# Spectral mixing and SwiGLU on one core: the transforms' first step on 32x32 parts of folded rows, its stores from SyncE

## The chip, the core and the metric

The kernel runs on one core of a Trainium2 chip, in fp32. The metric is the time of one execution on the device in microseconds (us), as the median of several runs. Engines are named as in the profile: PE is TensorE's matmul, PEld its weight load, DVE is VectorE, ACT is ScalarE, POOL is GpSimd, SP is SyncE. ACTq and SPq are the queues on which ACT and SP issue DMA transfers.

## The reference

Eight batches of 3008 tokens with 256 channels are filtered along the tokens and then go through a SwiGLU network with 1536 hidden columns:

```python
X = np.fft.rfft(x, axis=1)                     # x is (8, 3008, 256)
y = np.fft.irfft(X * (filt_r + 1j * filt_i)[None], n=3008, axis=1)
t = y.reshape(24064, 256)
g = t @ w_gate
out = (g / (1 + exp(-g)) * (t @ w_val)) @ w_out
```

## The kernel before, in words

Each batch is worked off in twelve steps: four token groups times three groups of hidden columns. A step runs through one list that is written out by hand, `SCHEDULE`, some 200 tokens long, and every engine keeps the order of its instructions in that list. The tokens that the text meets are these. `P`, `Q`, `A`, `B` and `E` are products of the gate and value matrices (L1075, PSUM tiles wk, wa, we). `W` is an output projection (L1172, tiles wA, wF, wG), and `o` adds such a tile into the output sums on DVE. `f`, `c`, `x`, `y`, `m`, `g`, `u`, `h` evict and combine the products (L1090 to L1122); `D` is such a combination on POOL. `z` transposes output sums. The large matmul work is cut by schemes of sums, so that a projection or a product has to wait for sums on DVE, ACT or POOL.

The filter of a batch is calculated while the network of the batch before it runs. Its transform is split over the factors 3008 = 47 x 64. A piece of that work is a generator, and each of the tokens `b0` to `b7` takes it on by one `yield`; these are the bursts. For batches from 2 on, steps 0 to 3 of the batch before hold `quads(0)` to `quads(3)`, the first step of the transform: 47-point sums down the rows, for two of the eight pieces of columns at a time. Each piece is 4 columns n of 256 channels, in two halves h that lie 32 columns apart. The burst b0 of a `quads` has eight matmuls (L716, PSUM tiles wqa), each with 47 rows times 64 results times 512 columns in a 64x64 part of the array; an fp32 matmul makes two passes, so the trace has 16 records. b1 and b2 each evict half h = 0 of a piece by an ACT copy (L725), then take the difference and the sum with half h = 1 on DVE (L331 and L328, helpers for all such sums). b3 and b4 store the pieces in DRAM from ACT's queue (L733), and `load_x` (L641) brings pieces for the next `quads` on SP. At b6 of step 3 `load_four` reads that DRAM tile for the second step of the transform, `fours`, which occupies steps 4 to 10 (matmuls L775 and L787); in it `keep` copies a PSUM tile on ACT (L801) and the copies' halves are swapped by DMA (the raw swaps). Scratch rows for all this lie in one tile, `lent`, and `room_of(tag)` gives the part of a tag (x, f, y, g, e, t).

PSUM tiles named w share seven banks in rotation: what asks for a bank waits until the reader of the bank's previous tile is done.

SP issues nearly all other transfers in the program's order, a transfer that has to wait holding those behind it. `reload_weights` (L493) brings the weights of the next step in pieces of 896 and 768 KB, each when PE is done with the piece it replaces. In batch 1, at places in steps 0 to 2 (`FILTER_AT`), `keep_filter` arranges the filter in DRAM, and `negated_filter` makes a copy of part of it with the sign turned: loads, an ACT multiplication (L323, 64x1024), and stores. Batch 0 takes other paths for its own transform and has weight preparation beside it; chores are pieces of work placed at a step and a token of batch 0.

Of the kernel before, what the change touches and what calls it, by code (L numbers as in the profile page):

```python
# [41 lines left out]
FP32 = mybir.dt.float32  # L42
# [57 lines left out]
S00 S01 W1 S20 S21 S10 S11 W5 o1 W2 o5 S30 S31 W6 o2 z0.o o6 W3 o3 z1.o x0.o x1.o x2.o x3.o x4.o  # L100
x5.o W7 q4 o7 z3.o W4 o4 z2.o X0.o X1.o X2.o X3.o X4.o X5.o
""".split()
FILTER_AT = ("f1", "P0", "Q2", "h0", "g3", "A12", "Q0", "P1", "c1", "h1")
BLOCKS = (0, 1, 3, 2)
PAIRS = ((0, 1), (1, 2), (2, 3), (0, 2), (1, 3), (0, 3))
PAIRS_USED = ((1, 3), (0, 1), (0, 2), (1, 2), (2, 3), (0, 3))
# [19 lines left out]
def dft_tables():  # L126
# [37 lines left out]
            if n >= NH:  # L164
                back[row:row + rows, first + N1 * i:first + N1 * (i + 1)] = one_hi[a:a + rows]

    quad = np.zeros((128, 64))
    for h, turn in enumerate((ph, ph + 2 * np.pi * s / (2 * N1))):
        cols = np.stack([np.cos(turn), -np.sin(turn)], 2).reshape(N1, 2 * NS)
        quad[64 * h:64 * h + N1, 0:2 * NS] = cols  # L170

    four = np.zeros((128, N_FOUR + 1, 2, 4, 64))
    lo, qq = np.arange(32), np.arange(32)
# [32 lines left out]
def kernel(  # L206
# [60 lines left out]
    def weights_of(b, k, g):  # L267
        return wt_1 if b == 0 and k < NT and g == 1 else wt_t

    dram_tiles = [wdpool.tile([2 * NS, N2, C], FP32, name=f"d{1 + i % 2}_{i // 2}")  # L270
                  for i in range(4)]
    yt_dram = [wdpool.tile([128, 3 * len(PAIRS), TQ], FP32, name=f"yt_{k}") for k in range(NT)]
    y_dram = [wdpool.tile([128, 8, TQ], FP32, name=f"y_{k}") for k in range(NCHUNK)]
    o_dram = [wdpool.tile([128, 4 * NH, RP], FP32, name=f"o_{k}") for k in range(NT)]
# [32 lines left out]

    def keep_filter(n):

        part, r, e, half = (0, 0, 1)[n // 4], (0, 1, 1)[n // 4], n // 2 % 2, n % 2  # L310
        q = 32 * e + 16 * half
        pin(nc.sync.dma_start(out=f_pairs[q:q + 16, r, part],
                              in_=filter_rows(part, e, half, 0, NS)))

    def negated_filter(w, stage):

        t = room_of("et"[w % 2])[0:64].rearrange("p (s c) -> p s c", c=C)
        if stage == 0:
            for q in range(4):
                pin(nc.sync.dma_start(out=t[16 * q:16 * q + 16],  # L320
                                      in_=filter_rows(1, q // 2, q % 2, 4 * w, 4)))
        elif stage == 1:
            pin(nc.scalar.mul(t, t, -1.0))  # L323
        else:
            pin(nc.sync.dma_start(out=f_pairs[:, 0, 1, 4 * w:4 * w + 4], in_=t))

    def add(eng, dst, a, b):
        return eng.tensor_tensor(out=dst, in0=a, in1=b, op=ALU.add)  # L328
# [246 lines left out]
    def load_back():  # L575

        t = rpool.tile([128, 2, 128], U32, name="quad", tag="pw", bufs=3)
        t = t.bitcast(FP32).rearrange("p b f -> p (b f)")
        quad_t.append(t)
        pin(nc.sync.dma_start(out=t[:, 0:64], in_=quad_dram.ap()))  # L580
# [19 lines left out]
    class Spectral:  # L600


        def __init__(self, b):
            self.b = b
            self.d1, self.d2 = [dram_tiles[2 * (b % 2) + i] for i in range(2)]
# [23 lines left out]
        def load_x(self, u):  # L629
            if self.b == 0:  # L630
                rows = x[0].rearrange("(r n) c -> r n c", n=32)
                for a, n in ((0, 4), (4, 4)):
                    for r in (slice(0, 80), slice(80, NR)):
                        self.load(out=x0[u][r, a:a + n, :],
                                  in_=rows[r, 8 * u + a:8 * u + a + n, :])
            elif self.b > 1:
                if u < N_QUAD:
                    self.x[u] = room_of("x", u).rearrange("p (n c) -> p n c", c=C)
                    rows = x[self.b].rearrange("(r n) c -> r n c", n=N2)
                    for h in range(2):  # L640
                        for a, e in ((0, 32), (32, N1)):  # L641
                            self.load(out=self.x[u][64 * h + a:64 * h + e],
                                      in_=rows[a:e, 32 * h + 4 * u:32 * h + 4 * u + 4])
            elif u < N_ONE:
                self.x[u] = xpool.tile([NR, NV, C], FP32, name=f"x_{self.b}_{u}", tag="x")
                rows = x[self.b].rearrange("(r n) c -> r n c", n=32)

                for r in (slice(0, 80), slice(80, NR)):
                    self.load(out=self.x[u][r], in_=rows[r, ts(u, NV), :])
# [49 lines left out]
        def bank(self, name):  # L699
# [2 lines left out]
                return bank(name).rearrange("p (i c) -> p i c", i=NV)  # L702
            return fbank(name)

        def quads(self, g):

            pieces = (2 * g, 2 * g + 1)
            banks = {}
            for u in pieces:
                xt = self.x.pop(u)  # L710
                for h in range(2):
                    banks[u, h] = bank(f"qa_{self.b}_{u}_{h}")
                for cp in range(2):
                    for h in range(2):
                        r = slice(64 * h, 64 * h + N1)
                        pin(nc.tensor.matmul(  # L716
                            out=banks[u, h][64 * cp:64 * cp + 64], lhsT=quad_t[0][r, 0:64],
                            rhs=xt[r, 2 * cp:2 * cp + 2].rearrange("p n c -> p (n c)"),
                            start=True, stop=True))
            yield  # L720
            t1 = {u: room_of("yg"[i]).rearrange("p (n h c) -> p n h c", h=2, c=C)
                  for i, u in enumerate(pieces)}
            for u in pieces:
                low, high = [banks[u, h].rearrange("p (n c) -> p n c", c=C) for h in range(2)]
                pin(nc.scalar.copy(out=t1[u][:, :, 0], in_=low))  # L725
                pin(sub(nc.vector, t1[u][:, :, 1], t1[u][:, :, 0], high))
                pin(add(nc.vector, t1[u][:, :, 0], t1[u][:, :, 0], high))
                yield
            d1 = self.d1.rearrange("a (n h) c -> a n h c", h=2)
            for u in pieces:  # L730
                for cp in range(2):
                    n = 4 * u + 2 * cp
                    pin(nc.scalar.dma_start(out=d1[:, n:n + 2], in_=t1[u][64 * cp:64 * cp + 2 * NS]))  # L733
                self.load_x(u + 2)
                yield
            if g == 3:
                self.load_filter(0)
                self.load_turns(0)
            yield
            if g == 3:  # L740
                self.load_four(0)

        def load_four(self, w):

            if w < N_FOUR:
                t = self.t2[w] = room_of("t").rearrange("p (s h c) -> p s h c", h=2, c=C)
                d1 = self.d1.rearrange("(s r) (n h) c -> s (r n) (h c)", r=2, h=2)
                for p in range(2):
                    s = 4 * w + 2 * p
                    self.load(out=t[64 * p:64 * p + 64].rearrange("p s h c -> p s (h c)"),  # L750
                              in_=d1[s:s + 2].rearrange("s q c -> q s c"))

        def load_filter(self, w):

# [10 lines left out]
        def fours(self, w):  # L765
# [32 lines left out]
            def keep(p):  # L798
                t = t1pool.tile([128, NV, C], FP32, name=f"raw_{self.b}_{w}_{p}", tag="t1", bufs=2)
                raw.append(t)  # L800
                pin(nc.scalar.copy(out=t, in_=there[p]))  # L801

            def real(p):
                a = slice(2 * p, 2 * p + 2)
# [576 lines left out]
    for b in range(B):  # L1381
# [36 lines left out]
        for step in range(NCHUNK * NG + (b == B - 1)):  # L1418
# [16 lines left out]
            for place, token in enumerate(SCHEDULE):  # L1435
# [31 lines left out]
                    continue  # L1467
                if b == 0 and (step, op) == (5, "A23"):
                    nxt.load_two(0)
                if b + 2 < B and (step, op) in ((11, "Q2"), (11, "B01")):  # L1470
                    following.load_x(int(op == "B01"))
                if b == 1 and step < 4 and op in FILTER_AT:
                    n = FILTER_AT.index(op)
                    if n < 4 and step < 3:
                        keep_filter(4 * step + n)
                    elif 4 <= n < 6 and step < 3:
                        negated_filter(2 * step + n % 2, 0)
                    elif n >= 6 and step:
                        negated_filter(2 * step - 2 + n % 2, n // 2 - 2)
# [43 lines left out]
```

## Time and profile before

| what | us |
|---|---|
| median of 3 runs | 2821.29 |
| lowest and highest run | 2817.37, 2822.79 |
| the profiled execution's own time | 2823.7 |
| its span, first to last instruction | 2821.6 |
| mean granted TensorE clock | 0.997 |
| PE busy in the span | 2787.5 |
| DVE, ACT, POOL busy | 1999.1, 1564.7, 1579.9 |
| DMA moved | 586.59 MB, mean 208 GB/s |
| PE busy from 60 to 430 us (batch 0) | 352.6 of 370 |
| PE busy from 430 to 2805 us | 2373.4 of 2375 |

Busy times of the engines lie beside each other and do not add up to the span. A line of the timeline gives start and duration in us, engine, source line and operation, then output and inputs by their names, partitions and sizes, the number of instructions that the line joins, and in brackets how long the engine had been idle and what released it. In the chain of waits a line gives start, duration, engine, operand and source line.

### The profile page before, as it was taken

The page shows a single profiled execution, that of the slowest core. Times are in us where ns is not written, and L with a number is a line of the kernel's source. Part 1 is how long each engine was busy: PE and PEld are TensorE (multiplying, and loading weights), DVE is VectorE, ACT ScalarE, POOL GpSimd, SP SyncE. Part 2 cuts the span into 40 slices and gives each one's busy share as a digit, 9 for nine tenths or more (in the row PEclk, how much of TensorE's full clock was granted, in tenths as well). Part 3 has the DMA queues.
Part 4 walks back from the last instruction along what each step waited for, and adds up shares of the span by engine and source line. Part 5 has one row for each costly group of instructions (what it writes and reads, how often), then busy time and mean ns, then how long its engine had stood idle before and what let it go on. Part 6 is the DMA issues. An engine that isn't in the chain of part 4 may idle for free.

```text
span 2821.6 us, 48540 instructions
## 1 busy us (share of the span) xinstructions
PE 2787.5 (99%) x15444; PEld 2319.9 (82%) x15444; DVE 1999.1 (71%) x4579; ACT 1564.7 (55%) x4176; POOL 1579.9 (56%) x1689
## 2 busy tenths in 40 slices
PE   8999999999999999999999999999999999999998
PEld 6877888888888888788888888878888888888887
DVE  7898767767667766667766677667676767666666
ACT  5675455555555555555555555555555555555554
POOL 4786576465545565456653566445655455545544
PEclk9999999999999999999999999999999999999999
DMA  9687876877666775667666676667766677654443
GB/s 214 224 272 237 283 242 211 285 233 232 181 188 207 246 221 175 204 215 229 222 185 197 211 246 201 188 190 236 228 205 181 213 224 227 192 153 148 153 137 82
DMA packets 362933, 586.59 MB, mean 208 GB/s; under 512 B 198620, under 2 KB 245660, under 8 KB 362536
## 3 DMA queue, kind: packets, MB, share of 16 engines
q1 hardware_dynamic: 337722, 533.61, 60.8%
q10 hardware_dynamic: 22318, 44.38, 5.7%
q0 software_dynamic: 2640, 5.51, 0.7%
q8 instruction: 125, 2.05, 0.3%
q14 instruction: 128, 1.05, 0.1%
HBM read 467.48 MB, written 101.34 MB: 202 GB/s over the span
## 4 chain that ended last, share of the span: by engine, by line
PE 91%; POOL 2%; DVE 2%; DMA 1%; issue 1%; ACT 1%; ACTq 0%; SPq 0%; POOLq 0%; DVEq 0%
PE wa L1075 25%; PE wk L1075 17%; PE wA L1172 16%; PE we L1075 13%; PE wG L1172 8%; PE wF L1172 4%; PE pd L978 3%; PE wqa L716 2%; PE wqc L775 1%; PE wqb L787 1%; POOL out_dram L1157 0%; POOL h L331 0%; PE pa L857 0%; DMA lent<-later_tbl 0%; PE pd L981 0%
## 5 line engine op out<-in xcount | busy, mean ns | idle before, releaser
L1075 PE MATMUL wa<-y_t,wt_t 128*128 128x188 f32 x4464 | 881.6, 324 | 4.0 <-DVE wa L1097 2.3
L1075 PEld LDWEIGHTS wa<-y_t,wt_t 128*128 128x128 f32 x4464 | 749.8, 191 | 79.5 <-ACT wa L1101 9.3
L1075 PEld LDWEIGHTS wk<-y,wt_t 128*128 128x128 f32 x2976 | 495.0, 190 | 109.5 <-issue 33.4
L1075 PE MATMUL wk<-y,wt_t 128*128 128x188 f32 x2976 | 572.0, 325 | 3.2 <-ACT f L1090 3.2
L331 POOL TENSOR_TENSOR h<-h 128x376 f32<-128x376 f32 x572 | 559.6, 1000 | 15.4 <-DVE h L328 15.2
L328 POOL TENSOR_TENSOR h<-h 128x376 f32<-128x376 f32 x190 | 182.8, 983 | 685.5 <-DVE h L1122 685.5
L1172 PE MATMUL wA<-h,wo_t 128*128 128x376 f32 x1532 | 551.8, 482 | 3.9 <-DVE o L328 2.1
L1075 PE MATMUL we<-y_t,wt_t 128*128 128x188 f32 x2232 | 431.7, 323 | 1.6 <-ACT we L1106 1.5
L331 POOL TENSOR_TENSOR D<-f,f 128x376 f32<-128x376 f32 x288 | 280.0, 986 | 258.4 <-ACT f L1090 256.0
L331 DVE TENSOR_TENSOR we<-we,m 128x376 f32<-128x376 f32 x576 | 319.8, 556 | 141.1 <-PE we L1075 73.9
L1075 PEld LDWEIGHTS we<-y_t,wt_t 128*128 128x128 f32 x2232 | 369.3, 190 | 2.7 <-ACT we L1106 2.1
L1172 PEld LDWEIGHTS wA<-h,wo_t 128*128 128x128 f32 x1532 | 274.9, 190 | 113.7 <-issue 7.0
L1110 ACT COPY m<-wa 128x376 f32<-128x376 f32 x576 | 272.7, 473 | 102.0 <-PE wa L1075 98.8
L335 DVE SCALAR_TENSOR_TENSOR y<-wk,c 128x376 f32<-128x376 f32 x480 | 244.8, 541 | 63.8 <-ACT c L1094 37.8
L1117 ACT ACTIVATE g<-wa 128x188 f32<-128x188 f32 x576 | 187.5, 326 | 164.7 <-PE wa L1075 154.9
L1117 ACT ACTIVATE u<-we 128x188 f32<-128x188 f32 x576 | 188.7, 328 | 160.2 <-DVE we L331 153.3
L1172 PE MATMUL wG<-h,wo_t 128*128 128x376 f32 x768 | 274.0, 479 | 0.0
L1094 ACT COPY c<-wk 128x376 f32<-128x376 f32 x288 | 136.5, 474 | 226.0 <-PE wk L1075 196.7
L1090 ACT ACTIVATE f<-wk 128x376 f32<-128x376 f32 x288 | 140.4, 488 | 168.6 <-PE wk L1075 118.0
L1106 ACT COPY we<-y 128x376 f32<-128x376 f32 x480 | 222.3, 480 | 19.8 <-DVE h L1122 14.4
L1122 DVE TENSOR_TENSOR h<-wa,g 128x188 f32<-128x188 f32 x576 | 199.4, 347 | 38.0 <-ACT g L1117 37.6
L1122 DVE TENSOR_TENSOR h<-we,u 128x188 f32<-128x188 f32 x576 | 198.5, 345 | 28.8 <-ACT u L1117 17.3
(193 smaller groups left out, 3523.0 us busy)
## 6 DMA issues: line engine op xcount, KB each, us to landing
wt_t<-w_all SPq DMA_DIRECT2D x174, 896.0 KB
wt_t<-w_all SPq DMA_DIRECT2D x174, 768.0 KB
lent<-filter SPq DMA_DIRECT2D x36, 1024.0 KB
lent<-d SPq DMA_DIRECT2D x84, 256.0 KB
d<-lent ACTq DMA_DIRECT2D x84, 256.0 KB
d<-lent ACTq DMA_DIRECT2D x96, 192.0 KB
lent<-raw SPq DMA_DIRECT2D x144, 128.0 KB
t<-d SPq DMA_DIRECT2D x114, 128.0 KB
```

The costliest lines, as they stand in the source:

```text
L328: return eng.tensor_tensor(out=dst, in0=a, in1=b, op=ALU.add)
L331: return eng.tensor_tensor(out=dst, in0=a, in1=b, op=ALU.subtract)
L335: return nc.vector.scalar_tensor_tensor(out=dst, in0=a, scalar=-1.0, in1=b, op0=ALU.mult, op1=ALU.subtract)
L978: pin(nc.tensor.matmul(out=rows, lhsT=self.t4[k, i][:, j, ts(cb, 128)], rhs=cols, start=j == 0, stop=True, skip_group_check=True))
L1075: pin(nc.tensor.matmul(out=ps[:, z], lhsT=self.wt[:, SLOT[p], z], rhs=rhs, start=start and z == 0, stop=True, skip_group_check=True))
L1090: pin(act.mul(self.small(f"f{i}", f"f{i}", 1), t[f"k{i}"], -1.0))
L1094: pin(act.copy(out=self.small(f"c{i}", f"c{i}", 1), in_=t[f"k{i}"]))
L1106: pin(act.copy(out=self.bank(f"e{at}"), in_=t[f"y{at}"]))
L1110: pin(act.copy(out=self.small(f"m{at}", "m", 4), in_=t[f"a{at}"]))
L1117: pin(act.activation(out=self.small(op, "g", 3, 1)[:, 0], in_=ps[:, 1], func=AF.Silu))
L1122: pin(v.tensor_tensor(out=dst, in0=ps[:, 0], in1=g, op=ALU.mult))
L1172: pin(nc.tensor.matmul(out=self.tiles[at], lhsT=wo_t[:, JB * q + i, WO[p], :], rhs=self.hs[i][:, HID[p]], start=start and i == 0, stop=Tru ...
```

## The change

From batch 2 on, the sums over 47 rows are done on rows that are folded first. Row r and row 47-r are added and subtracted, so that 24 rows of sums and 24 rows of differences remain. The sums serve the real results, the differences the imaginary ones. Each part is 24 rows by 24 results and fits a 32x32 part of the array. The constant matrix `quad` gets that form, and a 65th column of +1 and -1.

The rising rows are loaded by four transfers of 128 KB. The falling rows are reversed by transfers from DRAM to DRAM (`turn_rows`, into `turned_dram`), as chores in batch 0 for batch 2 and at step 8, token Q0, of later batches; one transfer of 512 KB then loads them. `load_x(0)` stands at (11, Q0), the other three inside `fold`. `fold(g)` has four DVE operations of 128x512, from SBUF to SBUF, at b4 to b7 of the step before its `quads(g)`.

`quads(g)` takes pieces g and g+4. Its burst b0 has 16 matmuls of 24 rows, 32 results and 512 columns. b1 has the ACT copy, difference and sum of its first piece, b2 the ACT copy of the second, and b3 the second's difference and sum. b5 stores both pieces from SP (64 partitions, 256 KB each of four transfers) in new DRAM tiles, `quads_dram`. `load_four` stays at b6 of step 3 with four loads of 32 partitions. `negated_filter` is gone and `keep_filter` is called 16 times; the sign is applied in `keep`, by ACT with the new column as its scale.

```diff
-FILTER_AT = ("f1", "P0", "Q2", "h0", "g3", "A12", "Q0", "P1", "c1", "h1")
+FILTER_AT = ("f1", "P0", "Q2", "h0")
...
-    quad = np.zeros((128, 64))
...
+    quad = np.zeros((4, 32, 2, 32))
+    for h in range(2):
+        turn = 2 * np.pi * (np.outer(2 * n1[0:NS] + h, s) % (2 * N1)) / (2 * N1)
+        quad[2 * h:2 * h + 2, 0:NS, 0, 0:NS], quad[2 * h:2 * h + 2, 0:NS, 1, 0:NS] = np.cos(turn), -np.sin(turn)
+        quad[2 * h:2 * h + 2, 23 * h] *= np.array([0.5, 0.0])[:, None]
+    quad = np.concatenate([quad.reshape(128, 64), np.tile([[1.0], [-1.0]], (64, 1))], 1)
...
-    def negated_filter(w, stage):
-
-        t = room_of("et"[w % 2])[0:64].rearrange("p (s c) -> p s c", c=C)
-        if stage == 0:
-            for q in range(4):
-                pin(nc.sync.dma_start(out=t[16 * q:16 * q + 16],
-                                      in_=filter_rows(1, q // 2, q % 2, 4 * w, 4)))
-        elif stage == 1:
-            pin(nc.scalar.mul(t, t, -1.0))
-        else:
-            pin(nc.sync.dma_start(out=f_pairs[:, 0, 1, 4 * w:4 * w + 4], in_=t))
...
-                if u < N_QUAD:
-                    self.x[u] = room_of("x", u).rearrange("p (n c) -> p n c", c=C)
+                if u < N_QUAD // 2:
+                    self.x[u] = [room_of("x", n) for n in range(2)]
+                    up, down = self.x[u]
+                    at = self.turned.rearrange("(g q) p c -> g p q c", q=4)[u]
+                    self.load(out=down.rearrange("p (q c) -> p q c", c=C), in_=at)
                     rows = x[self.b].rearrange("(r n) c -> r n c", n=N2)
-                    for h in range(2):
-                        for a, e in ((0, 32), (32, N1)):
-                            self.load(out=self.x[u][64 * h + a:64 * h + e],
-                                      in_=rows[a:e, 32 * h + 4 * u:32 * h + 4 * u + 4])
+                    for n in range(4):
+                        first = 16 * n + 4 * u
+                        self.load(out=up[ts(n, 32)].rearrange("p (q c) -> p q c", c=C),
+                                  in_=rows[0:32, first:first + 4])
...
+    def turn_rows(self, *parts):
+        xb, to = x[self.b], self.turned
+        end = NS if self.b > 3 else 32
+        for part in parts:
+            h, lane, n = part // 2, 32 * part, 16 * part
+            p = 1 - h
+            self.load(out=to[:, lane + p:lane + end],
+                      in_=bass.AP(tensor=xb.tensor, ap=[[C, 16], [-N2 * C, end - p], [1, C]],
+                                  offset=xb.offset + ((N1 - 1) * N2 + n) * C))
+            if h == 0:
+                self.load(out=to[:, lane], in_=xb[n:n + 16])
+
+    def fold(self, g):
+        if g < N_QUAD // 2:
+            up, down = self.x.pop(g)
+            self.x[g] = [room_of("e"), room_of("t")]
+            for t, f in zip(self.x[g], (add, sub)):
+                for half in range(2):
+                    a = ts(half, NV * C)
+                    pin(f(nc.vector, t[:, a], up[:, a], down[:, a]))
+                    if t is self.x[g][1] and half:
+                        self.load_x(g + 1)
+                    yield
...
     def quads(self, g):
-        pieces = (2 * g, 2 * g + 1)
...
+        pieces = (g, g + N_QUAD // 2)
+        banks = {(u, h): bank(f"qa_{self.b}_{u}_{h}") for u in pieces for h in range(2)}
+        parts = self.x.pop(g)
+        for cp in range(2):
+            for t in range(2):
+                for i, u in enumerate(pieces):
+                    for h in range(2):
+                        r, c = 32 * (2 * h + i), 32 * (2 * cp + t)
+                        pin(nc.tensor.matmul(
+                            out=banks[u, h][c:c + 32], lhsT=quad_t[0][r:r + NS, ts(t, 32)],
+                            rhs=parts[t][r:r + NS, ts(cp, NV * C)],
+                            start=True, stop=True))
+        yield
+        fold = self.fold(g + 1)
...
+        low(pieces[0])
+        both(pieces[0])
+        yield
+        low(pieces[1])
+        yield
+        both(pieces[1])
+        yield
+        next(fold, None)
+        yield
+        for u in pieces:
+            store(u)
         if g == 3:
             self.load_filter(0)
             self.load_turns(0)
+        next(fold, None)
         yield
         if g == 3:
             self.load_four(0)
+        next(fold, None)
+        yield
+        next(fold, None)
...
             def keep(p):
...
-                pin(nc.scalar.copy(out=t, in_=there[p]))
+                pin(nc.scalar.mul(t, there[p], quad_t[0][:, 64:65]))
...
+    for part, at in enumerate(((3, "E23"), (4, "A13"), (4, "E23"), (5, "A13"))):
+        chore(*at, lambda part: following.turn_rows(part), part)
...
+        if b + 2 < B:
+            bursts[-1] = following.first_fold()
...
-                if b + 2 < B and (step, op) in ((11, "Q2"), (11, "B01")):
-                    following.load_x(int(op == "B01"))
+                if b and b + 2 < B and (step, op) == (8, "Q0"):
+                    following.turn_rows(0, 1, 2, 3)
+                if b + 2 < B and (step, op) == (11, "Q0"):
+                    following.load_x(0)
```

`low` is the ACT copy, `both` the difference and the sum, `store` two transfers of a piece on SP, and `first_fold` lets four bursts pass before `fold(0)`.

More of the change, by code (lines that the diff above doesn't have):

```diff
@@ L165, in dft_tables @@
                 back[row:row + rows, first + N1 * i:first + N1 * (i + 1)] = one_hi[a:a + rows]
-    quad = np.zeros((128, 64))
-    for h, turn in enumerate((ph, ph + 2 * np.pi * s / (2 * N1))):
-        cols = np.stack([np.cos(turn), -np.sin(turn)], 2).reshape(N1, 2 * NS)
-        quad[64 * h:64 * h + N1, 0:2 * NS] = cols
+    quad = np.zeros((4, 32, 2, 32))
[4 more added lines that the diff above has]
+    quad = np.concatenate([quad.reshape(128, 64), np.tile([[1.0], [-1.0]], (64, 1))], 1)
     four = np.zeros((128, N_FOUR + 1, 2, 4, 64))
@@ L271 @@
                   for i in range(4)]
+    quads_dram = [wdpool.tile([64, N2, C], FP32, name=f"quads_{i}") for i in range(2)]
+    turned_dram = [wdpool.tile([16, 128, C], FP32, name=f"turned_{i}") for i in range(2)]
     yt_dram = [wdpool.tile([128, 3 * len(PAIRS), TQ], FP32, name=f"yt_{k}") for k in range(NT)]
@@ L308, in keep_filter @@
     def keep_filter(n):
-        part, r, e, half = (0, 0, 1)[n // 4], (0, 1, 1)[n // 4], n // 2 % 2, n % 2
+        part, r, e, half = n // 8, n // 4 % 2, n // 2 % 2, n % 2
         q = 32 * e + 16 * half
@@ L579, in load_back @@
         quad_t.append(t)
-        pin(nc.sync.dma_start(out=t[:, 0:64], in_=quad_dram.ap()))
+        pin(nc.sync.dma_start(out=t[:, 0:65], in_=quad_dram.ap()))
         t = rpool.tile([128, 2, 128, 2], U32, name="back", tag="raw", bufs=2)
@@ L604, in __init__ @@
             self.b = b
+            self.quads_dram, self.turned = quads_dram[b % 2], turned_dram[b % 2]
             self.d1, self.d2 = [dram_tiles[2 * (b % 2) + i] for i in range(2)]
@@ L703, in bank @@
             return fbank(name)
-        def quads(self, g):
-            pieces = (2 * g, 2 * g + 1)
[L708 to L719, printed above, removed]
+        def turn_rows(self, *parts):
[9 more added lines that the diff above has]
+                    self.load(out=to[:, lane], in_=xb[n:n + 16])
@@ new lines, in first_fold @@
+        def first_fold(self):
+            for _ in range(4):
+                yield
+            yield from self.fold(0)
+        def quads(self, g):
+            pieces = (g, g + N_QUAD // 2)
[10 more added lines that the diff above has]
+                                start=True, stop=True))
@@ L720, in quads @@
             yield
+            fold = self.fold(g + 1)
             t1 = {u: room_of("yg"[i]).rearrange("p (n h c) -> p n h c", h=2, c=C)
                   for i, u in enumerate(pieces)}
[L723 to L728, printed above, removed]
@@ L729, in quads, with low, both @@
-            d1 = self.d1.rearrange("a (n h) c -> a n h c", h=2)
-            for u in pieces:
+            views = {key: t.rearrange("p (n c) -> p n c", c=C) for key, t in banks.items()}
+            def low(u):
+                pin(nc.scalar.copy(out=t1[u][:, :, 0], in_=views[u, 0]))
+            def both(u):
+                pin(sub(nc.vector, t1[u][:, :, 1], t1[u][:, :, 0], views[u, 1]))
+                pin(add(nc.vector, t1[u][:, :, 0], t1[u][:, :, 0], views[u, 1]))
+            d1 = self.quads_dram.rearrange("a (n h) c -> a n (h c)", h=2)
@@ L731, in quads, with store @@
+            def store(u):
                 for cp in range(2):
                     n = 4 * u + 2 * cp
-                    pin(nc.scalar.dma_start(out=d1[:, n:n + 2], in_=t1[u][64 * cp:64 * cp + 2 * NS]))
-                self.load_x(u + 2)
-                yield
+                    self.load(out=d1[:, n:n + 2], in_=t1[u][64 * cp:64 * cp + 64])
+            low(pieces[0])
[4 more added lines that the diff above has]
+            both(pieces[1])
@@ L746, in load_four @@
                 t = self.t2[w] = room_of("t").rearrange("p (s h c) -> p s h c", h=2, c=C)
-                d1 = self.d1.rearrange("(s r) (n h) c -> s (r n) (h c)", r=2, h=2)
+                d1 = self.quads_dram.rearrange("(r s) (n h) c -> r n s (h c)", r=2, h=2)
                 for p in range(2):
                     s = 4 * w + 2 * p
-                    self.load(out=t[64 * p:64 * p + 64].rearrange("p s h c -> p s (h c)"),
-                              in_=d1[s:s + 2].rearrange("s q c -> q s c"))
+                    for r in range(2):
+                        a = 64 * p + 32 * r
+                        self.load(out=t[a:a + 32].rearrange("p s h c -> p s (h c)"),
+                                  in_=d1[r, :, s:s + 2])
         def load_filter(self, w):
@@ L1469 @@
                     nxt.load_two(0)
-                if b + 2 < B and (step, op) in ((11, "Q2"), (11, "B01")):
-                    following.load_x(int(op == "B01"))
+                if b and b + 2 < B and (step, op) == (8, "Q0"):
+                    following.turn_rows(0, 1, 2, 3)
+                if b + 2 < B and (step, op) == (11, "Q0"):
+                    following.load_x(0)
                 if b == 1 and step < 4 and op in FILTER_AT:
                     n = FILTER_AT.index(op)
[L1474 to L1479, printed above, removed]
+                    keep_filter(4 * step + n)
                 if b and chunk and op == "B01":
```

## The prediction

> **What bounds the kernel now.** First the page's busy times and its chain of waits.
>
> ```profile
> PE 2787.5 (99%) x15444; PEld 2319.9 (82%) x15444; DVE 1999.1 (71%) x4579; ACT 1564.7 (55%) x4176; POOL 1579.9 (56%) x1689
> ...
> PE 91%; POOL 2%; DVE 2%; DMA 1%; issue 1%; ACT 1%; ACTq 0%; SPq 0%; POOLq 0%; DVEq 0%
> ```
>
> TensorE (PE) is busy for 99%, and the chain stays on it for 91%: removed PE time is a gain if nothing else takes its place. From 449.6 us to 2805 us PE stands still in two places only, both behind the stores of quads; the chain of waits has them:
>
> ```profile
> 540.18 2.75 ACTq L733
> ...
> 1194.10 1.68 ACTq L733
> ```
>
> ScalarE's (ACT's) queue was held by a store, an ACT copy came late, and PE stood still for 1.42 us at 543.3 and 0.49 us at 1197.1 (PE's timeline).
>
> Then PE's timeline at step 0 of batch 2, the first of the 24 steps with such a block:
>
> ```profile
> 790.62 1.95 PE L716 MATMUL wqa<-lent,quad 47*64 47x512 f32 x16
> 792.50 1.54 PE L1075 MATMUL wk<-y,wt_t 128*128 128x188 f32 x8
> 793.93 1.50 PE L1172 MATMUL wA<-h,wo_t 128*128 128x376 f32 x4
> ...
> 799.71 1.44 PE L1075 MATMUL wa<-y_t,wt_t 128*128 128x188 f32 x8
> ```
>
> Eight matmuls, two fp32 passes each, hold PE from 790.62 to 792.50: 1.88 us, the same in all 24 blocks, 45.1 us in all. The weight loads show the rounds:
>
> ```profile
> 790.62 0.21 PEld L716 LDWEIGHTS wqa<-lent,quad 47*64 47x64 f32 x8 [0.53 <-issue]
> 791.10 0.15 PEld L716 LDWEIGHTS wqa<-lent,quad 47*64 47x64 f32 x4 [0.28 <-issue]
> 791.53 0.15 PEld L716 LDWEIGHTS wqa<-lent,quad 47*64 47x64 f32 x4 [0.28 <-issue]
> ```
>
> Four records start 7 ns apart (the first line joins two rounds), the next four 0.43 us later: four rounds of four 64x64 tiles.
>
> Last, VectorE (DVE) behind that block, from its timeline:
>
> ```profile
> 792.38 0.69 DVE L331 TENSOR_TENSOR lent<-lent,wqa 128x512 f32<-128x512 f32 x1 [3.00 <-ACT lent L725]
> 793.10 0.69 DVE L328 TENSOR_TENSOR lent<-lent,wqa 128x512 f32<-128x512 f32 x1
> ...
> 795.94 0.54 DVE L328 TENSOR_TENSOR o<-o,wA 128x376 f32<-128x376 f32 x1
> 796.51 0.55 DVE L328 TENSOR_TENSOR o<-o,wF 128x376 f32<-128x376 f32 x1
> ...
> 798.29 0.55 DVE L1097 SCALAR_TENSOR_TENSOR wa<-wk,D 128x376 f32<-128x376 f32 x1
> ...
> 800.71 0.55 DVE L1097 SCALAR_TENSOR_TENSOR x<-wk,D 128x376 f32<-128x376 f32 x1 [0.72 <-ACT g L1117]
> ```
>
> From 792.38 to 799.99 DVE has no hole. Its last wa<-wk,D ends at 798.84, and PE needs it at 799.71: 0.87 us of margin. A shorter block moves PE forward against this row; that decides what survives.
>
> **What the Trainium skill says.** "TensorE: Matmul & The Clock Gate", Part 3 (packing small matmuls), gives for sixteen tiles of K=M=32, N=512 one matmul's time plus about 4 ns per further tile. The trace agrees in kind (four tiles 7 ns apart, one round for all) and shows no sixteen. "TensorEngine Tiling (Array Packing)", PSUM Bottleneck, warns that evacuation may bound once tiling has made TensorE faster: agreed, the margin of wA at 793.93 to the sum that frees its bank (793.78) is 0.15 us. "DMA: Bandwidth & Descriptors", the SWDGE anatomy, states that a DMA's semaphore wait is served on the issuing sequencer: agreed, the 2.75 us above.
>
> **The change, part by part.**
>
> *The block.* Sixteen matmuls in 32x32 tiles, two passes, are 32 records; with sixteen at once, two rounds instead of four: −2×0.43, +0.08 for twelve more starts of 7 ns in a round. 1.88 becomes 1.10, 0.78 us saved; ×24 = **18.7 us** at most. The mode switches around the block stay.
>
> *Folds.* For each of the 24 blocks four 128x512 sums or differences from SBUF to SBUF join DVE. Row L845 has this shape: 682 ns, about 0.60 us in sequence since neighbours overlap; 2.4 us a step, 58 us over the kernel. They stand at bursts b4 to b7 of the step before (11, 0, 1, 2). DVE's busy share there, from the window table, is 22.0 of 29.2 us, 18.3 of 29.2 and 19.6 of 27.6 (steps 0 to 2), so there is room in sum; order decides.
>
> Step 0: DVE's first difference waits for the ACT copy, 0.07 us later than before relative to wk's start. The second pair of sums moves behind x and wa (b3), so those are 1.2 us earlier, and the pair ends near 796.1 on the old clock; then o, a fold (0.60), o, transpose, y, h; wa<-wk,D ends near 799.45 instead of 798.84 (one fold more, one gap less). PE, advanced by 0.78, is there at 798.93 and waits until some 0.06 after that end, 799.51, where it was at 799.71 before: of 0.78 only **0.2 us** survives. wA now waits for the second ACT copy, which isn't later.
> Step 1: DVE idles 1.22 us before y and 1.77 us before x in the same stretch; they take the folds: **0.77**.
> Step 2: idle 0.54 us before y, then a slack of 0.19 us on wa<-x: **0.65**.
> Step 3: no fold, the pair moved: **0.75**.
> Step 11: fold(0) into idles of 0.65 and 0.79 us, with 1.9 us of PE margin behind: nothing.
> Sum 2.37 us a batch, ×6 = **14.2 us**.
>
> *Stores.* 192 KB ×4 from ACT become 256 KB ×4 from SyncE (SP) at b5. ACT's two holes go: **−1.9 us** (1.42 + 0.49). On SP the stores wait for sums of b3; behind them stand weight pieces, raw swaps and, in step 3, load_four at b6. SP's own waits are already long (9.6 us was the longest for a weight piece) and load_four's result has about 12 us: nothing. What was late behind the holes is next the same ACT chain, without delay.
>
> *Signs.* 72 copies become ACTIVATE with a scale: f's ACTIVATE takes 488 ns, c's COPY 474: +14 ns ×72 = 1 us on an ACT that idles 11 to 13 us a step: nothing. Dropping negated_filter takes six 1057 ns multiplications off ACT and 24 loads and stores off SP in batch 1, against four more keep_filter loads: nothing visible, since PE did not stall there.
>
> *Loads of x.* Eight loads a step become five (512 KB of turned rows, 4×128 KB). The first is issued at (11, Q0), near 759.3, behind 768 KB of weights that flow until 762.5. 512 KB in 1 KB packets at 240 KB/us (192 such packets in a us at 757), shared, and 512 KB more at 400 KB/us: landing near 766. fold(0) is wanted at 765.95; it may be late by its idle and margin, 2.5 us. Nothing. Of the other three pieces each has most of a step.
>
> *Turned rows.* In step 8 six copies in DRAM, 2 MB, about 8.5 us at 240 KB/us, with a DMA share of 0.70 there. The raw swaps queued behind them land up to 10 us later and are needed about 13 us on: nothing, bound 0 to +1 us a batch. In batch 0 four of 512 KB fall between 170 and 260 us, where the DMA share is 0.93 and 0.83, and PE waits there for transfers already: no row prices it. Four copies of 2.1 us each on all engines are 8.5 us; half of that on PE's path is +4, none is 0. I take **+1**, as most transfers there are not the one PE waits for, and keep both ends.
>
> Sum: −14.2 −1.9 +1 = **−15.1 us** against the profiled execution's 2823.7, that is 2808.6. It lay 2.4 above the median of 2821.29; the median becomes **2806**.
>
> **Rivals.**
> *Half an overlap.* Three rounds instead of two: 0.43 saved a block; (0.2 + 3×0.43)×6 = 8.9, +1.9 −1 = 9.8: 2812. For: no row shows over four tiles at once. Against: passes of different tiles run together in rounds of 7 ns steps.
> *VectorE or x becomes the bound.* If folds wait for late x, or the moved pair holds the bank chain, the b4 to b7 rows stand before products in DVE's order and PE waits. What steps 0 to 2 save is eaten: 1.62×6 = 9.7 us, and the gain falls to 5.4, give or take 2: 2814 to 2818. For: the seamless 7.6 us of DVE in step 0. Against: the holes of steps 1 and 11.
> *Slower: only four matmuls in flight.* If PE admits just four small matmuls, and a group's second passes run beside the next group's first ones, the block takes five rounds: 1.88 + 0.43 = 2.31 us. 24×0.43 = 10.4, −1.9 +1 = +9.5: near 2831. It decides from the point where a block passes 1.88 us. For: the trace never has more than four at once, and the before block would look the same under it. Against: the packing that the skill states.
> *No effect.* The folds and the DRAM copies, or blocks that stay at four rounds, give back all that is saved: 2821.
>
> **How the numbers follow.** Forecast 0.62 (2801 to 2811: all of 18.7 + 1.9 survives, or 4 us go to DRAM copies), half an overlap 0.13, DVE or x 0.09, four in flight 0.13, no effect 0.03. 0.2% is 5.6 us, about what a measurement of this kernel can tell from no change: below 2815.7 it is faster. The first two cases and a third of the third (0.03), a little over in tails, make 0.79 faster; the rest of the third with no effect 0.08 same; four in flight 0.13 slower. The range reaches from 2798 (everything survives, and the unlisted ACT margins give 3 us) to 2819, the third case's end; what lies above is 0.15.
>
> **What would show it.** Right: the wqa block near 1.10 us, 32 records in two groups sixteen strong; step 0 of each batch shorter by 0.2 us, step 1 to 3 by 0.65 to 0.8; no ACTq piece at quads' stores in the chain; four more rows of 0.68 us on DVE; no new PE wait behind SP. Wrong: a block of 1.5 or 2.3 us (rounds of four or eight), PE waits on wa or wA with DVE as releaser in steps 0 to 2, DMA as releaser of a fold, or a longer stretch between 170 and 260 us.

## The result, and the profile after

The changed kernel takes 2813.93 us (median of 20 runs, 2810.15 to 2821.05), the kernel before 2820.07 us beside it (20 runs). The ratio is 0.9979 with an interval of 0.9972 to 0.9986: 6.1 us faster, where 15 had been forecast. The profiled execution took 2812.9 us, with a span of 2811.1.

The page's busy times and the shares of the chain, after:

```profile
PE 2774.9 (99%) x15828; PEld 2310.4 (82%) x15828; DVE 2050.7 (73%) x4675; ACT 1560.3 (56%) x4170; POOL 1580.6 (56%) x1689
...
PE 91%; DVE 3%; POOL 2%; ACT 1%; DMA 1%; issue 0%; SPq 0%; POOLq 0%; ACTq 0%; DVEq 0%
```

DVE has 51.6 us more, and its share of the chain went from 2% to 3%, while PE's stayed at 91%: PE now waits for DVE in places where it did not before. The weight loads and PE's timeline at step 0 of batch 2:

```profile
789.13 0.23 PEld L743 LDWEIGHTS wqa<-lent,quad 24*32 24x32 f32 x32 [0.53 <-issue]
```

```profile
789.13 1.14 PE L743 MATMUL wqa<-lent,quad 24*32 24x512 f32 x32
790.20 1.75 PE L1123 MATMUL wk<-y,wt_t 128*128 128x188 f32 x8
791.79 1.43 PE L1220 MATMUL wA<-h,wo_t 128*128 128x376 f32 x4
...
798.02 1.54 PE L1123 MATMUL wa<-y_t,wt_t 128*128 128x188 f32 x8 [0.36 <-DVE wa L1145]
```

The block is as forecast: 1.07 us from its start to wk, against 1.88. Its 32 single records, which these lines join, start in two groups of 16, 7 ns apart in a group and the second group 0.45 us after the first. What is new is the last line: PE waits for DVE. DVE's timeline in the same step shows why:

```profile
791.02 0.69 DVE L323 TENSOR_TENSOR lent<-lent,wqa 128x512 f32<-128x512 f32 x1 [3.14 <-ACT lent L754]
...
795.04 0.68 DVE L320 TENSOR_TENSOR lent<-lent 128x512 f32<-128x512 f32 x1
...
797.41 0.55 DVE L1145 SCALAR_TENSOR_TENSOR wa<-wk,D 128x376 f32<-128x376 f32 x1
```

From 791.02 to the end of wa<-wk,D at 797.96 there is no hole, and the fold at 795.04 stands in it. PE goes on at 798.02, 0.52 us after its own pace. In step 2 another fold stands ahead of we<-wk,c; first DVE's timeline, then the weight loads behind it:

```profile
863.14 0.68 DVE L323 TENSOR_TENSOR lent<-lent 128x512 f32<-128x512 f32 x1
863.74 0.55 DVE L327 SCALAR_TENSOR_TENSOR we<-wk,c 128x376 f32<-128x376 f32 x1
```

```profile
864.35 0.62 PEld L1123 LDWEIGHTS we<-y_t,wt_t 128*128 128x128 f32 x4 [0.34 <-DVE we L327]
```

The same fold stands ahead of we<-wk,c in step 0, where it costs less; DVE's timeline, then the weight loads:

```profile
806.64 0.68 DVE L323 TENSOR_TENSOR lent<-lent 128x512 f32<-128x512 f32 x1
```

```profile
807.85 0.62 PEld L1123 LDWEIGHTS we<-y_t,wt_t 128*128 128x128 f32 x4 [0.16 <-DVE we L327]
```

Laying the two kernels' PE instructions side by side, from block to block, gives the account by step. It is the same in batches 2 to 6 to within 0.02 us, but for one longer step of the kernel before (28.21 at 1188.96 instead of 27.6, the hole of 0.49 that the prediction named):

| from block to block, us | before | after | change | forecast |
|---|---|---|---|---|
| step 0 | 29.21 | 29.24 | +0.03 | -0.20 |
| step 1 | 29.21 | 28.48 | -0.73 | -0.77 |
| step 2 | 27.60 | 27.22 | -0.38 | -0.65 |
| step 3 and on | 253.91 | 253.45 | -0.46 | -0.75 |
| sum, a batch | | | -1.54 | -2.37 |
| batch 1: steps 0, 1, 2, 3 and on | 29.21, 29.07, 27.47, 255.29 | 29.24, 29.80, 28.07, 254.40 | +0.47 in all | -2.37, and -1.4 of hole |

Batch 1 is the surprise: steps 1 and 2 are longer than before. PE's timeline there has a wait that no later batch has:

```profile
480.31 1.50 PE L1220 MATMUL wA<-h,wo_t 128*128 128x376 f32 x4 [0.63 <-DVE lent L320]
```

wA waits for the sum of the first piece on DVE (lent, L320), since it uses the PSUM bank which that sum frees; it starts 3.45 us after the block instead of the 2.66 of later batches, 0.79 us behind, and as much in steps 2 and 3.

### The profile page after: what moved, and what is told of

Same layout as the page of the kernel before. It is cut to its first block, busy times and chain, and to the rows that moved or that the text cites. A ratio compares the mean times of both kernels' runs of the same rounds, so it can differ in the third digit from the quotient of the medians.

```text
span 2811.1 us, 49259 instructions
## 1 busy us (share of the span) xinstructions
PE 2774.9 (99%) x15828; PEld 2310.4 (82%) x15828; DVE 2050.7 (73%) x4675; ACT 1560.3 (56%) x4170; POOL 1580.6 (56%) x1689
## 4 chain that ended last, share of the span: by engine, by line
PE 91%; DVE 3%; POOL 2%; ACT 1%; DMA 1%; issue 0%; SPq 0%; POOLq 0%; ACTq 0%; DVEq 0%
PE wa L1123 25%; PE wk L1123 17%; PE wA L1220 17%; PE we L1123 12%; PE wG L1220 8%; PE wF L1220 4%; PE pd L1026 3%; PE wqc L823 1%; PE wqb L835 1%; PE wqa L743 1%; POOL h L323 0%; POOL out_dram L1205 0%; DMA lent<-later_tbl 0%; PE pc L980 0%; PE pa L905 0%
## 5 line engine op out<-in xcount | busy, mean ns | idle before, releaser
L320 POOL TENSOR_TENSOR h<-h 128x376 f32<-128x376 f32 x190 | 182.7, 982 | 686.8 <-DVE h L1170 686.8
```

## The experiments

"After the first block" below is the stretch from the start of the first block to the last instruction of the profiled execution: 2372.1 us before, 2363.5 after. It leaves out batch 0, whose length varies.

**Thin folds.** Is it the folds?

```diff
+                        a = slice(a.start, a.start + 8)
                         pin(f(nc.vector, t[:, a], up[:, a], down[:, a]))
```

> Changed kernel with each fold operation on 8 columns instead of 512, at the same places; most of the folding is left out, so the result is not the reference's. Theory A (VectorE's order): of the 0.8 us that a block saves, the folds take back most where one stands ahead of a product's sum, 0.62 us in step 0 (the fold in front of wa<-wk,D), 0.14 in step 0 and 0.32 in step 2 (the fold in front of we<-wk,c). [...]from batch 2 on step 0 goes from 29.24 to about 28.5, step 2 from 27.22 to about 26.9, steps 1 and the rest stay within 0.05; about 1.0 us a batch, 6 us in all. Theory B (the block ends in one piece, so the first ACT copy and VectorE's chain start 0.14 us later and that chain itself is too long): step 0 gains less than 0.3 and step 2 nothing.

Measured from batch 2 on: 28.62, 28.48, 26.87, 253.46; after the first block 2357.1, 6.4 us less; ratio to the kernel before 0.9951 (0.9938 to 0.9965). A thin fold still takes 0.17 to 0.26 us on DVE in the mean, instead of 0.68. Steps 0 and 2 get 0.62 and 0.35 us shorter and the others stay. Theory A holds: the folds cost PE 0.97 us a batch, all of it in two steps. Of B only a rest remains: without full folds, too, wa in step 0 follows wa<-wk,D and falls back by 0.14.

**Moved folds.** Is it the number of the folds or their places?

```diff
             both(pieces[1])
             yield
-            next(fold, None)
             yield
...
-            next(fold, None)
-            yield
-            next(fold, None)
+            next(fold, None)
+            self.late_fold = fold
...
+                if b and nxt and step < 3 and op in ("h12", "u13"):
+                    next(nxt.late_fold, None)
```

> Changed kernel with two of the four folds of steps 0 to 2 moved to late places in the same step, after h12 and after u13, where VectorE idles 0.4 to 0.8 us; the other two stay at b5 and b6. Theory A: the same gain as with thin folds, about 0.6 to 0.75 us in step 0 and 0.3 in step 2, if the late places cost PE nothing; 5 to 6 us in all. Theory B: under 0.3 us a batch, and where the late places are as tight as the early ones, steps 1 and 2 get longer by up to 0.3 each.

Measured: 28.62, 28.48, 26.87, 253.46, the same as with thin folds, with all the folding done; after the first block 2357.4; ratio 0.9955 (0.9940 to 0.9969). DVE's and then PE's timeline at step 0 of batch 2 in this kernel, whose block starts at 786.21:

```profile
793.32 0.51 DVE L327 SCALAR_TENSOR_TENSOR y<-wk,c 128x376 f32<-128x376 f32 x1
793.75 0.34 DVE L1168 TENSOR_TENSOR h<-wk,g 128x188 f32<-128x188 f32 x1
794.01 0.55 DVE L1143 SCALAR_TENSOR_TENSOR wa<-wk,D 128x376 f32<-128x376 f32 x1
```

```profile
793.94 0.80 PE L1121 MATMUL wk<-y,wt_t 128*128 128x188 f32 x4
794.62 1.54 PE L1121 MATMUL wa<-y_t,wt_t 128*128 128x188 f32 x8
```

Without the fold ahead of it wa<-wk,D ends at 794.56, 8.35 us after the block instead of 8.83, and PE goes from wk to wa with no wait in the line, though with the same rest of 0.14 as under thin folds. So all the folding, 51.6 us of DVE's busy time, costs PE no more than thin folds do; it was two places in the order that cost 6 us.

**Turned eviction in batch 1.** Is the wait of wA there the bank's?

```diff
-            low(pieces[0])
-            both(pieces[0])
+            first, second = pieces if self.b > 2 or not g else pieces[::-1]
+            low(first)
+            both(first)
             yield
-            low(pieces[1])
+            low(second)
             yield
-            both(pieces[1])
+            both(second)
```

> Changed kernel; in steps 1 to 3 of batch 1 alone the two pieces of quads change places in the eviction, so that the projection wA there gets a bank that an ACT copy frees, as it does in all later batches, and not one that VectorE's sum frees. Theory C (banks): the three waits of 0.79 us of wA in batch 1 go, 2.4 us in all, the intervals between its blocks become those of later batches (28.5, 27.2 within 0.3), and nothing changes from batch 2 on. Rival (batch 1 has other waits, from the filter's transfers or from its projections): they stay at 29.80 and 28.07.

Measured in batch 1: 29.24, 28.51, 27.26, 253.49; later batches unchanged; after the first block 2360.5, 3.0 us less; ratio 0.9965 (0.9951 to 0.9979). PE's timeline at step 1 of batch 1:

```profile
479.00 1.14 PE L743 MATMUL wqa<-lent,quad 24*32 24x512 f32 x32
480.07 1.78 PE L1124 MATMUL wk<-y,wt_t 128*128 128x188 f32 x8
481.69 1.43 PE L1221 MATMUL wA<-h,wo_t 128*128 128x376 f32 x4
```

The wait is gone and the intervals are those of the other batches within 0.04. In the changed kernel wA had the first piece's bank that DVE's sum frees; here it waits for an ACT copy, as in later batches. The bound of 2.4 us was too low by 0.6: in step 1 a wait of we for we<-wk,c, 0.45 us, went with the bank's.

**Piece order.** The same cause the other way round: the order of the 16 matmuls alone moves the banks.

```diff
-            for cp in range(2):
-                for t in range(2):
-                    for i, u in enumerate(pieces):
-                        for h in range(2):
+            for i, u in enumerate(pieces):
+                for cp in range(2):
+                    for t in range(2):
+                        for h in range(2):
```

> Changed kernel with the 16 matmuls of a block in another order: all eight of the first piece ahead of the second's. The banks that the pool then hands out put wA in all batches, not only in batch 1, on the bank that VectorE's sum of the first piece frees. Theory C (banks): wA waits about 0.79 us in every one of the 24 steps; from batch 2 on steps 1 and 3 get 0.6 to 0.8 us longer (28.48 to about 29.2), step 0 less, since its later wait for wa<-wk,D takes in part of it; 10 to 15 us slower than the changed kernel. Rival (wA's wait in batch 1 came from the order of eviction itself): batches from 2 on stay within 0.1 us a step. The block itself should stay at 1.07 us with two groups of 16.

Measured, now in all batches alike: 29.38, 29.25, 27.98, 253.96; after the first block 2373.8, 10.3 us more than the changed kernel; the one execution took 2820.74. PE's timeline at step 1 of batch 2:

```profile
815.11 1.14 PE L743 MATMUL wqa<-lent,quad 24*32 24x512 f32 x32
816.18 1.65 PE L1123 MATMUL wk<-y,wt_t 128*128 128x188 f32 x8
818.46 0.87 PE L1220 MATMUL wA<-h,wo_t 128*128 128x376 f32 x2 [0.63 <-DVE lent L320]
```

The block is unchanged at 1.07 us and the wait of batch 1 now stands in every step. In this single execution an order of 16 matmuls, through the banks that follow from it, costs more than the whole change brought.

**Sums early.** What is the move of the second piece's sums to b3 worth?

```diff
             low(pieces[1])
-            yield
             both(pieces[1])
             yield
+            yield
```

> Changed kernel with the second piece's difference and sum at b2 again, ahead of x and wa13 on VectorE. If the move to b3 carries part of the gain: x and wa13 end 1.3 us later, wa13 is wanted 5.0 us after the block and comes at about 5.5, so each step from batch 2 on gets 0.3 to 0.6 us longer, but for step 0, where the later wait for wa<-wk,D takes that in; 6 to 10 us in all. If the move carries nothing: all steps within 0.1 us.

Measured: 29.24, 29.00, 27.71, 253.90; after the first block 2370.3, 6.8 us more; ratio to the kernel before 0.9998 (0.9989 to 1.0006). DVE's timeline in step 1 of batch 2, and PE's behind it:

```profile
819.65 0.68 DVE L323 TENSOR_TENSOR lent<-lent,wqa 128x512 f32<-128x512 f32 x1
820.36 0.69 DVE L320 TENSOR_TENSOR lent<-lent,wqa 128x512 f32<-128x512 f32 x1
820.97 0.54 DVE L1145 SCALAR_TENSOR_TENSOR x<-wk,f 128x376 f32<-128x376 f32 x1
821.42 0.55 DVE L1145 SCALAR_TENSOR_TENSOR wa<-wk,f 128x376 f32<-128x376 f32 x1
```

```profile
822.03 0.90 PE L1123 MATMUL wa<-y_t,wt_t 128*128 128x188 f32 x4 [0.25 <-DVE wa L1145]
```

With the old order of sums PE stands before this product (wa13) in steps 1 to 3, 0.5 us each, and the shorter block with its folds brings nothing that could be told from zero.

**Stores on ACT.** What is the move of the stores worth?

```diff
-                    self.load(out=d1[:, n:n + 2], in_=t1[u][64 * cp:64 * cp + 64])
+                    pin(nc.scalar.dma_start(out=d1[:, n:n + 2], in_=t1[u][64 * cp:64 * cp + 64]))
```

> Changed kernel with the stores of quads issued from ACT again, at b5 and b6's neighbour as now, in place of SyncE. The pool's hand-out of banks in batch 1 becomes that of the later batches. Theory C (banks): batch 1 gets 3 us shorter. Theory E (stores on ACT hold up its queue): ACT stands 2 us or more behind a store in each of the 24 steps, and where that reaches PE, single steps from batch 2 on are longer by 0.3 to 1.5 us. Rival: ACT idles 11 us a step, the stores cost nothing in any step, and the kernel is 3 us faster than the changed one.

Measured: 30.9, 30.06, 28.91, 254.6; after the first block 2398.2, 34.7 us more; median 2850.74, ratio to the kernel before 1.0102 (1.0086 to 1.0117). ACT's timeline at step 1 of batch 3:

```profile
1145.30 3.05 ACTq L765 DMA_DIRECT2D quads<-lent  x4
1148.38 0.48 ACT L1041 COPY y<-pd 128x376 f32<-128x376 f32 x1 [2.76 <-DMA quads<-lent]
```

Four stores in a row hold ACT for 3.05 us, evictions stand behind them, and PE waits for ACT and DVE before we. Theory E holds, and beyond its size: the steps are longer by 1.1 to 1.7 us. At this place ACT cannot issue the stores without holding up PE; the kernel before issued its smaller stores at b3 and b4, and its PE stood still behind them in two places only. Theory C holds too, though the intervals of batch 1 (30.94, 31.05) are covered by E: in its steps 1 and 2 wA starts 2.66 us after the block, as in later batches, and not at 3.45. So the wait of batch 1 came with the move of the stores to SP.

**Copies alone.** Do the DRAM copies hold up batch 0? `turn_rows` and its four chores were added to the kernel before, and nothing else.

```diff
+    for part, at in enumerate(((3, "E23"), (4, "A13"), (4, "E23"), (5, "A13"))):
+        chore(*at, lambda part: following.turn_rows(part), part)
```

> Kernel before with nothing added but the four copies of turned rows in batch 0 (2 MB from DRAM to DRAM, read by nobody). Theory D (the copies hold up batch 0): the medians differ by only 6.1 us between the kernels before and after, while from the first block on the profiles differ by 8.6; the 2.5 us between lie in batch 0, and this kernel is 2 to 3 us slower than before, its first block later by as much. Rival (they lie beside other work, and the start of a run varies by some us): within 1 us of before.

Measured: 2819.52 us against 2819.36, ratio 0.9997 (0.9989 to 1.0006). Theory D fell. From the first wk to the first block batch 0 takes 375.5 us before, 375.3 after and 374.2 here, and between 371.8 and 377.3 in all the kernels' profiles. But this kernel showed where the odd 2 us lie: it issues the same stores from ACT as the kernel before, and its chain has no ACTq piece from the first block on. After the first block it takes 2370.1 us, not 2372.1. The two holes belonged to the one profiled execution of before more than to the kernel. Against 2370.1 the changed kernel's 2363.5 is 6.6 us less, which agrees with 6.1 of the medians.

**Both repairs.** Moved folds and turned eviction together.

> Changed kernel with both repairs: two folds at late places (after h12 and u13) and the eviction order of batch 1's steps 1 to 3 turned. If the two causes add, the stretch from the first block to the end is 2363.5 - 6.1 - 2.5 = 2355 us (the folds in batch 1 have part of their cost in waits that the banks hide), and the median lies near 2805, 9 us below the changed kernel and 15 below the kernel before. If they overlap, the second repair brings under 1 us: 2807.

Measured: from batch 2 on as with moved folds, batch 1 28.63, 28.51, 26.91; after the first block 2355.5; median 2805.72, ratio 0.9937 (0.9925 to 0.9950). The causes add as expected; with the next kernel, of equal time, this is the fastest version, 15 to 17 us below the kernel before. A batch gains 2.51 us, where 2.37 had been forecast for the changed kernel.

**Step 3's late copy.** In step 3 the first ACT copy starts 1.41 us after the block's start, in steps 0 to 2 at 1.28, and the second wk tile, which waits for it, is later by as much. The weight loads in steps 0 and 3 of the changed kernel, batch 2, with step 3's wait for wa<-wk,D last:

```profile
791.04 0.62 PEld L1123 LDWEIGHTS wk<-y,wt_t 128*128 128x128 f32 x4 [0.23 <-ACT lent L754]
...
876.11 0.62 PEld L1123 LDWEIGHTS wk<-y,wt_t 128*128 128x128 f32 x4 [0.36 <-ACT lent L754]
...
882.60 1.25 PEld L1123 LDWEIGHTS wa<-y_t,wt_t 128*128 128x128 f32 x8 [0.16 <-DVE wa L1145]
```

In the kernel with both repairs, step 3 alone got another order of the block's matmuls:

```diff
+            inner = [(t, i, h) for t in range(2) for i in range(2) for h in range(2)]
+            for cp, t, i, h in ([(cp, *n) for cp in range(2) for n in inner] if g < 3 else
+                                [(cp, t, i, h) for t in range(2) for cp in range(2)
+                                 for i in range(2) for h in range(2)]):
```

> Kernel with both repairs (late folds, turned eviction in batch 1), and in step 3 alone the block's matmuls take all that read the sums before all that read the differences. What it is to tell apart: in step 3 the first ACT copy starts 1.40 us after the block's start, in steps 0 to 2 at 1.28, though the matmuls start at the same distances. Theory F (signals): only in step 3 do several matmuls of the block's second half signal one behind the other, since the rooms of sums and differences are given to others there; with the new order these signals move, and the copy starts at about 1.28 to 1.30, so step 3 and what follows goes from 253.45 to about 253.2. Rival (something else on ACT or its rooms): the copy stays at 1.40 and the interval at 253.45. At most 0.25 us a batch, 1.5 us in all.

Measured: the copy stays at 1.41 (1.44 in batch 1), and the interval at 253.45 where nothing else disturbs it; ratio to the kernel before 0.9945 (0.9928 to 0.9962). Theory F fell for this order. In the kernel with the piece order the copy starts at 1.18 in all 24 steps, step 3 too, so it does hang on the order of the 16 matmuls; by what, stays open.

## Why the prediction was wrong, point by point

What failed is two prices. The first is that of the places in DVE's order, in steps 0, 2 and 3: the 2.37 us a batch came to 1.54, mainly because the prediction checked DVE's rows against too few of the sums that PE waits for (we<-wk,c above all) and put the later start of the first ACT copy at nothing. The second is that of the banks, which it did not look up for batch 1: "wA now waits for the second ACT copy" does not hold there. These two took 7.6 of the 15.1 us.

- **The block.** Right: 0.81 us saved instead of 0.78, two groups of 16. "Four in flight" and "half an overlap" did not come. The starts are 7 ns apart, not the 4 ns that the Trainium skill gives in "TensorE: Matmul & The Clock Gate", Part 3; that a further tile adds only a short step to the span fits: sixteen tiles start within 0.10 us. The gaps at the block's ends, which the prediction calls mode switches, stayed (weight loads idle 0.53 us ahead and 0.84 behind, against 0.53 and 0.81); what fills them is not shown.
- **Step 0.** The wait for wa<-wk,D came as forecast, with its size: 799.45 on the old clock is 8.83 us after the block's start, and there it ended; the first wa starts 0.2 us earlier than before. (DVE's chain starts 0.13 later against the block's start, not 0.07, and makes up for it; against wk's start, as the prediction has it, it is 0.94 later.) The 0.23 that failed lie behind this wait. The second wa matmul follows the first by 0.26 us instead of 0.16, which costs 0.10, for a reason that stays open. The last fold, ahead of we<-wk,c, was not counted: 0.14.
- **Step 2.** The step that failed is the slack: the prediction took 0.19 on wa<-x and did not look at we<-wk,c, ahead of which it put the fourth fold. Forecast -0.65, measured -0.38. Thin and moved folds both give -0.73.
- **Step 3.** Forecast -0.75, measured -0.46. The second wk tile waits for the first ACT copy, which is later against the block's start than before: when wA starts, 0.60 is left of the 0.81. Then wa<-wk,D is late and takes 0.14. The prediction said of the second copy that it is not later and did not ask about the first one. In the other steps the later copy costs 0.08.
- **Banks.** The step "wA now waits for the second ACT copy" was carried from later batches to batch 1, where wA got another bank. Missed: 3.0 us, shown by the turned eviction and, the other way round, by the piece order. The stores-on-ACT kernel shows that it came with the stores' move to SP, whose cost the prediction had put at nothing.
- **Stores.** The -1.9 us was read from a single execution. An ACT queue held by a store is what that trace shows, but it is a stall that comes and goes: the store that took 2.75 us (the median of the 96 is 0.44) names no semaphore that it waits for, and the same stores gave no such piece in another execution. What held it stays open. As a term of the sum it was worth little.
- **Copies in batch 0.** +1 was taken and 0 found; 2 MB of copies lay beside other work.
- **Fold (0), loads of x, turned rows in step 8, SP's order.** Costed at nothing. Fold (0) stands up to 2.3 us waiting for x in step 11, within the 2.5 us that it could bear, and no PE time is lost there. (SP's longest wait for a weight piece before was 10.0 us, not 9.6; nothing hung on it.)

The account: 15.1 forecast; less 0.83 for each of six batches, 5.0; less 2.6 in batch 1 beside that (its four intervals add up to 1.1 us above those of the copies-alone kernel, against -1.5 in later batches); less about 1.9 for holes; plus 1 for the copies: 6.6, against 6.1 measured. The rival "VectorE becomes the bound" described best what happened: rows of folds stand before products in DVE's order. That its 5.4 us lie so near is in part luck. It let steps 0 to 2 lose all that they save, while step 1 kept its 0.73 from batch 2 on; x was not what came late; and a good part of the loss was a bank in batch 1, freed by a sum that had not moved.

## What to carry to other kernels

When a shorter block moves PE forward, go through every product behind it and ask which row on DVE or ACT ends last before it; a new operation costs what it delays there, not its own duration, and moving two operations in a hand-written order brought as much again as the whole change had. Which PSUM bank a tile gets is part of the schedule: look it up for each stage, since a swap of two banks cost up to 0.8 us a step here. A stall seen in one execution is not a term of the sum until a second execution shows it.

## What the runs showed of the hardware

A fold has two inputs in SBUF. Alone it takes 0.68 us. 20 of the 96 folds took 0.79 to 1.42 us; 19 of these ran beside a POOL tensor operation, of the other 76 two did. DVE's timeline in step 0 of batch 2, then POOL's:

```profile
802.04 1.19 DVE L320 TENSOR_TENSOR lent<-lent 128x512 f32<-128x512 f32 x1
```

```profile
800.73 1.95 POOL L323 TENSOR_TENSOR h<-h 128x376 f32<-128x376 f32 x2
```

The Trainium skill gives a reason in "SBUF — State Buffer", SBUF: two separate sides: a DVE operation with two SBUF inputs and a POOL operation that reads SBUF take turns on one pair of ports, for whole instructions. The trace agrees: the second of these POOL operations runs until 802.68, 0.64 us into the fold, and the fold takes 0.51 us more than alone. The row from which the prediction took 682 ns had no such neighbour.

The ACTIVATE whose scale comes from a column of SBUF is slower than the copy of the same size that it replaced, by 95 ns and not by the 14 of the forecast. The sign in `keep` after, and the copy before:

```profile
L849 ACT ACTIVATE raw<-wqb,quad x72: 678/684/687, 563.7 to 2400.8; 128x512 f32<-128x512 f32 x72
```

```profile
L801 ACT COPY raw<-wqb x72: 586/589/592, 565.5 to 2410.6; 128x512 f32<-128x512 f32 x72
```

That is 6.8 us of ACT over the kernel; from the first block on no wait of PE of 0.2 us or more follows from it.
